# Spectral components stored from GpSimd's queue and read back behind their own store, and one block of matmuls moved ahead of the transposes

## Chip, cores and metric

One Trainium2 chip, one core. The time is that of the device in microseconds, from an execution's start to its end; the span in a profile leaves out some 2 us of that. Each kernel has several executions, and one of them is profiled. In the trace of the kernel before, TensorE does the matmuls (5826) and leaves their sums in the buffer PSUM; VectorE (679 instructions), ScalarE (487) and GpSimd (114) work on tiles; SyncE only issues transfers (the 14 stores of 512 KB among them), and ScalarE (4 stores of 256 KB) and GpSimd (8 stores of the filter) issue some too.

## The reference

```python
x = A_x                                             # 2048 x 1024, bf16
x = x + irfft2(rfft2(layernorm(x)) * (w_r + 1j*w_i))  # spectral layer
x = x + mish(layernorm(x) @ w1 + b1) @ w2             # dense layer, 1024 -> 3584 -> 1024
x = x + irfft2(rfft2(layernorm(x)) * (w_r + 1j*w_i))
x = x + mish(layernorm(x) @ w1 + b1) @ w2
```

## The kernel before

The transforms are matmuls with tables. A spectral layer works in 8 groups of frequencies. Stage s2 and s3 go forward, then comes the filter, then i1 and i2 go back. Each group leaves 128 x 16 x 128 components (512 KB) in a buffer U. The last transform, i4, needs them with all groups side by side in the partitions, so each group's U is stored to memory and read back in another order, in 256-byte pieces (2048 packets a group in the trace). A transfer is issued by an engine's queue. SyncE's works in its program's order: in experiment 5 it stood for 5 us until a store had landed, with the next store behind it.

```python
def u_turn(g, half):                      # after i2 of (group, half)
    u = U[g % 3]
    if g == 7:                            # last group, in two halves, ScalarE's queue
        h = slice(8 * half, 8 * half + 8)
        if half == 0:
            u_back(6)
        self.dma(act, self.u_d[g][:, h, :], u.ap[:, h, :], ...)
        if half:
            u_last()                      # read-backs of group 7 in six pieces, SyncE and ScalarE
    elif half:
        self.dma(sp, self.u_d[g], u.ap, ...)      # store, SyncE's queue
        if g:
            u_back(g - 1)                         # read-back of the group before, SyncE's queue
...
def layer_B(...):
    for u in range(4):
        self.i4(0, 4, 32 * u, 32, 2 * u)  # last transform, four quarters of 32 matmuls
        ...                               # ScalarE moves the sums from PSUM, VectorE takes statistics
    rest(0)                               # postponed block of 15 matmuls, PSUM banks 0 to 2
    for j in range(2):
        xn[j] = self.apply(j)             # VectorE normalises two tiles
    for j in range(2):
        transposed(0, j, xn[j])           # TensorE transposes, VectorE copies
    self.warm(ACT.Mish)                   # ScalarE loads a table (1.28 us)
    rest(3)                               # second block of 15, banks 3 to 5
    ...
        mm1(0, fg, 0, ...)                # dense matmuls
```

Of the kernel before, what the change touches and what calls it, by code (L numbers as in the profile page):

```python
# [179 lines left out]
class KB:  # L180
# [508 lines left out]
    def layer_A(self, li):  # L689
# [7 lines left out]
        dve, act, sp, pool = self.dve, self.act, self.sp, self.pool  # L697
# [166 lines left out]
        def u_turn(g, half):  # L864

            u = U[g % 3]
            if g == 7:
                h = slice(8 * half, 8 * half + 8)
                if half == 0:
                    u_back(6)  # L870
                self.dma(act, self.u_d[g][:, h, :], u.ap[:, h, :], f"uwh{half}", reads=[u.res], writes=[self.r_ud7[half]])
                if half:
                    u_last()
            elif half:
                self.dma(sp, self.u_d[g], u.ap, f"uw{g % 3}", reads=[u.res], writes=[self.r_ud[g]])
                if g:
                    u_back(g - 1)

        def open_ut():
            self.UT = self.alloc("UT", o["UT"], [P, P])  # L880

            self.r_ut = self.sub_res(self.UT, "ut", 4, o["UT"], P * P * 2)
            for r in self.r_ut:
                r.begin()

        def u_back(g):
            if self.UT is None:
                open_ut()
            self.dma(sp, self.UT.ap[g:P:8, :, :], self.u_d[g].rearrange("l r n -> r l n"), f"usp{g % 3}",
                     reads=[self.r_ud[g]], parts=self.r_ut)  # L890

        def u_last():

            def back(prog, half, q, n):
                l = slice(32 * q, 32 * q + 32 * n)
                self.dma(prog, self.UT.ap[7 + 64 * half:P if half else 64:8, l, :], self.u_d[7][l, 8 * half:8 * half + 8, :].rearrange("l r n -> r l n"),
                         f"ul{half}{q}", reads=[self.r_ud7[half]], parts=self.r_ut[q:q + n])
            back(sp, 0, 0, 2)
            back(sp, 0, 2, 2)
            for q in range(4):  # L900
                back((act, sp)[q % 2], 1, q, 1)
# [13 lines left out]
        for stage, g, h in self.order_A():  # L915
            if stage == 2:
                s2(g, h)
                if li == 0 and h == 0:
                    filter_bins(g)
                    if g in (0, 1):  # L920
                        load_w(g + 4)
                    elif g in (4, 5):
                        load_w(g + 2)
            elif stage == 3:
                s3(g, h)
                if h:
                    if g < 6:
                        load_tabs(g + 2)
                    if li == 0:
                        self.keep_filter(g)  # L930
                    elif g < 4:
                        load_w(g + 4)
            elif stage == 4:
                i1(g, h)
                if h and g < 6:
                    load_btabs(g + 2)
            else:
                i2(g, h)
                u_turn(g, h)
# [109 lines left out]
    def layer_B(self, li, last):  # L1049
        pe, dve, act, sp, pool = self.pe, self.dve, self.act, self.sp, self.pool  # L1050
# [109 lines left out]
        def at_tiles(c):  # L1160
            off = self.ob[f"AT{c}"]
            AT[c] = self.alloc(f"AT{c}", off, [NF, 512])
            r_at[c] = [Res(f"AT{c}_{ft}") for ft in range(NF)]
            for ft, r in enumerate(r_at[c]):
                r.inherit(AT[c].res)
                self.live.append((off + ft * 1024, off + ft * 1024 + 1024, r))

        def rest(bank, n=15, prog=act):

            u0 = self.u0  # L1170
            self.u0 += n
            self.i4(4, 12, u0, n, bank)
            self.i4_out(4, 12, u0, n, bank, staged=YS, prog=prog)
# [17 lines left out]
            self.out_first(u, 2, (act, act, act, dve)[u])  # L1191
        self.root(0, 2)
        rest(0)
        for j in range(2):
            xn[j] = self.apply(j)
        for j in range(2):
            transposed(0, j, xn[j])
        self.warm(ACT.Mish)
        rest(3)
        at_tiles(0)  # L1200
        for j in (2, 3):
            self.stats_dve(j)
# [118 lines left out]
```

## Time and profile before

| | before |
|---|---|
| time, first three runs | 1014.44, 1014.7, 1017.05 us |
| TensorE busy, share of the span | 95% |
| GpSimd busy | 8% |
| granted TensorE clock, mean | 0.992 |
| stores of 512 KB (SyncE's queue), to landing | 3.8 us |

The times of equal runs differ by 2.6 us. TensorE ran two stretches of together 17 us at half clock in this trace (granted clock 0.50 from 116.64 to 123.47 and from 604.75 to 614.99 us). The page's list of DMA issues has, for each kind of transfer, queue, count, size and median time from issue to landing:

```profile
u_scratch<-ARENA SPq DMA_DIRECT2D x14, 512.0 KB, 3.8
ARENA<-u_scratch SPq DMA_DIRECT2D x14, 512.0 KB, 6.1
```

TensorE's timeline at the first layer's turn (start, duration, line, shape, count; in brackets the idle time before and what ended it):

```profile
113.56 0.95 PE L1014 MATMUL PS<-MT,ARENA 128*128 128x32 bf16 x32 [1.62 <-DMA ARENA<-u_scratch]
115.35 2.88 PE L1014 MATMUL PS<-MT,ARENA 128*128 128x32 bf16 x96 [0.83 <-DMA ARENA<-u_scratch]
119.89 1.38 PE L1014 MATMUL PS<-MT,ARENA 128*128 128x96 bf16 x15 [1.67 <-ACT XS L568]
```

TensorE waits 1.67 us for ScalarE, and runs the first postponed block.

### The profile page before, as it was taken

To read this page: it belongs to the slowest core of one execution; us is meant where nothing else is said; L and a number is where in the kernel's file an instruction comes from. 1 tells how busy PE (TensorE), PEld (TensorE's weight loads), DVE (VectorE), ACT (ScalarE), POOL (GpSimd) and SP (SyncE) were. 2 spreads that over 40 slices of the span, in tenths; PEclk is the share of its full clock that TensorE was granted. 3 is DMA by queue.
4 is the path that set the end of the run, shared out by engine and by line. 5 is a ranking of instruction groups with operands and counts; after the bars stand their busy time and mean duration, and the time that the engine had idled before them with its cause. 6 is when DMAs were issued, how large, how long until landed. Compare 5 with 4: busy or idle time off the path is not lost.

```text
span 1013.4 us, 13752 instructions
## 1 busy us (share of the span) xinstructions
PE 958.2 (95%) x5826; PEld 506.4 (50%) x5826; DVE 326.5 (32%) x679; ACT 347.7 (34%) x487; POOL 81.5 (8%) x114
## 2 busy tenths in 40 slices
PE   0799799999999999999999979999999999999998
PEld 0667575444444444444456748644444444444443
DVE  6797568002444000033347736830011100000111
ACT  7798474440000443300029837534100023430000
POOL 3831000000000000002421100000000000000000
PEclk9999899999999999999999998999999999999999
DMA  9969823652111220002922875246411212100000
GB/s 281 281 191 321 213 60 115 198 196 65 48 46 32 74 82 21 1 21 85 199 60 84 232 187 154 77 161 203 129 25 45 73 52 83 43 1 11 21 27 26
DMA packets 154205, 107.00 MB, mean 106 GB/s; under 512 B 74448, under 2 KB 133664, under 8 KB 154144
## 3 DMA queue, kind: packets, MB, share of 16 engines
q1 hardware_dynamic: 143056, 78.61, 27.5%
q0 software_dynamic: 8912, 25.84, 8.7%
q10 hardware_dynamic: 2176, 1.66, 0.5%
q8 instruction: 47, 0.77, 0.3%
q14 instruction: 14, 0.11, 0.0%
HBM read 80.85 MB, written 20.71 MB: 100 GB/s over the span
## 4 chain that ended last, share of the span: by engine, by line
PE 87%; DVE 5%; DMA 4%; ACT 2%; POOL 1%; issue 0%; SPq 0%; ACTq 0%; POOLq 0%; DVEq 0%
PE PS L1121 38%; PE PS L1103 38%; PE PS L793 2%; PE PS L719 2%; PE PS L1014 2%; PE PS L818 2%; DMA XS<-in_A_x_dram 1%; DMA ARENA<-c_bt 1%; POOL ARENA L249 1%; PE PS L1069 1%; DMA ARENA<-u_scratch 1%; DVE ARENA L637 1%; DMA u_scratch<-ARENA 1%; DVE ARENA L775 1%; DVE ARENA L610 1%; ACT ARENA L635 1%
## 5 line engine op out<-in xcount | busy, mean ns | idle before, releaser
L1103 PE MATMUL PS<-ARENA 128*128 128x512 bf16 (+1 forms) x1984 | 390.9, 358 | 0.2
L1121 PE MATMUL PS<-ARENA 128*128 128x512 bf16 x1792 | 387.4, 379 | 0.0
L1107 ACT ACTIVATE ARENA<-PS,B 128x512 bf16<-128x512 f32 (+1 forms) x248 | 159.4, 645 | 411.6 <-PE PS L1103 411.0
L1103 PEld LDWEIGHTS PS<-ARENA 128*128 128x128 bf16 x1984 | 193.0, 98 | 192.7 <-DVE ARENA L1074 0.9
L1121 PEld LDWEIGHTS PS<-ARENA 128*128 128x128 bf16 x1792 | 175.4, 98 | 211.4
L1132 DVE TENSOR_TENSOR XS<-PS,XS 128x512 bf16<-128x512 f32 x63 | 43.6, 692 | 582.3 <-PE PS L1121 582.3
L460 DVE BATCH_NORM_STATS2 BN<-XS 128x6 f32<-128x512 bf16 x99 | 63.8, 673 | 6.1 <-DMA XS<-in_A_x_dram 5.1
L249 POOL DMA_DIRECT2D xn_scratch<-ARENA x12 | 6.5, 541 | 373.4 <-DVE ARENA L512 373.4
L793 PE MATMUL PS<-ARENA 128*128 128x256 bf16 x256 | 32.4, 273 | 3.9 <-DVE ARENA L782 3.2
L771 ACT ACTIVATE ARENA<-PS 128x1024 bf16<-128x1024 f32 x32 | 33.3, 1071 | 4.5 <-PE PS L767 4.5
L432 ACT ACTIVATE RS<-MV,EPS 128x2 f32<-128x2 f32 (+2 forms) x5 | 1.5, 297 | 96.6 <-DVE MV L463 84.4
L719 PE MATMUL PS<-FD,ARENA 128*128 128x256 bf16 (+1 forms) x256 | 31.8, 271 | 2.4 <-ACT ARENA L635 1.2
L1014 PE MATMUL PS<-MT,ARENA 128*128 128x32 bf16 (+1 forms) x512 | 22.3, 201 | 9.7 <-DMA ARENA<-u_scratch 6.3
L804 ACT ACTIVATE ARENA<-PS 128x1024 bf16<-128x1024 f32 x28 | 29.8, 1087 | 3.9 <-PE PS L793 3.9
L793 PEld LDWEIGHTS PS<-ARENA 128*128 128x128 bf16 x256 | 24.0, 98 | 12.0 <-DVE ARENA L782 5.7
L568 ACT ACTIVATE ARENA<-PS 128x1440 bf16<-128x1440 f32 (+1 forms) x22 | 25.5, 1160 | 10.8 <-PE PS L793 3.9
L775 DVE TENSOR_TENSOR ARENA<-ARENA 128x1024 bf16<-128x1024 bf16 x32 | 22.0, 688 | 19.8 <-ACT ARENA L771 19.8
L719 PEld LDWEIGHTS PS<-FD,ARENA 128*128 128x128 bf16 x256 | 24.4, 98 | 6.5 <-DVE ARENA L637 1.4
L1014 PEld LDWEIGHTS PS<-MT,ARENA 128*128 128x128 bf16 x512 | 20.6, 104 | 12.7 <-issue 7.2
L818 PE MATMUL PS<-ARENA,BD 128*128 128x256 bf16 x192 | 24.9, 273 | 1.6 <-DVE ARENA L572 1.6
L862 ACT ACTIVATE ARENA<-PS 128x1024 bf16<-128x1024 f32 x24 | 25.3, 1090 | 0.0
L512 DVE TENSOR_SCALAR ARENA<-XS,MV,RS 128x1024 bf16<-128x1024 bf16 x47 | 24.3, 543 | 0.9
(85 smaller groups left out, 530.6 us busy)
## 6 DMA issues: line engine op xcount, KB each, us to landing
ARENA<-in_B_w_dram SPq DMA_DIRECT2D x56, 512.0 KB, 3.9
ARENA<-in_B_w_dram SPq DMA_DIRECT2D x56, 256.0 KB, 4.3
u_scratch<-ARENA SPq DMA_DIRECT2D x14, 512.0 KB, 3.8
ARENA<-u_scratch SPq DMA_DIRECT2D x14, 512.0 KB, 6.1
w_scratch<-ARENA POOLq DMA_DIRECT2D x8, 512.0 KB, 6.9
ARENA<-w_scratch POOLq DMA_DIRECT2D x8, 512.0 KB, 5.3
out_dram<-XS SPq DMA_DIRECT2D x16, 256.0 KB, 2.1
ARENA<-xn_scratch POOLq DMA_DIRECT2D x15, 256.0 KB, 9.1
```

The source lines that it names most:

```text
L460: self.op(self.dve, lambda e: e.bn_stats(self.BN[:, j, 6 * h:6 * h + 6], self.XS[:, j, 512 * h:512 * h + 512]), reads=[self.r_xs[j]], part ...
L719: fns.append(lambda e: e.matmul(dst, at(r), FD[:, t:t + n], start=start, stop=stop))
L771: self.op(act, lambda e: e.activation(x.ap.rearrange("p a b -> p (a b)"), ps, ACT.Copy, scale=SIG), reads=banks, writes=[x.res])
L775: self.op(dve, lambda e: e.tensor_tensor(ta.ap, x.ap, wt.ap[:, 0:1, :].to_broadcast([P, 2, 512]), ALU.mult), reads=[x.res, wt.res], writes ...
L793: fns.append(lambda e, c=c, part=part: e.matmul(ps[:, c * 256:(c + 1) * 256], yk.ap[:, part, c * P:(c + 1) * P], t[:, (128, 0)[part]:(384, ...
L804: self.op(act, lambda e: e.activation(v.ap[:, :, i, :], src, ACT.Copy), reads=banks, parts=[v.res])
L818: fns.append(lambda e, dst=dst, part=part, c=c: e.matmul(dst, BD[:, c:c + P], mov(kd, part), start=(part == 0), stop=(part == 1)))
L1014: fns.append(lambda e, l=l: e.matmul(self.PS[:, bank + l // k, l % k * w:(l % k + 1) * w], self.UT.ap[:, u0 + l, :], self.MT[:, 8 * lo:8 * ...
L1103: fns.append(lambda e, db=db, bank=bank, fl=fl: e.matmul(PS[:, bank, 0:w], wb.ap[:, db, fl * P:(fl + 1) * P], x.ap[:, db, tok], start=(db ...
L1107: self.op(act, lambda e, bank=bank, ft=ft: e.activation(at.ap[:, ft, tok], PS[:, bank, 0:w], ACT.Mish, bias=self.B1[:, ft:ft + 1]), reads= ...
L1121: fns.append(lambda e, i=i, ft=ft: e.matmul(PS[:, bank, :], at.ap[:, ft, t * P:(t + 1) * P], W2[ft].ap[:, h * 512:(h + 1) * 512], start=(i ...
L1132: self.op(dve, lambda e: e.tensor_tensor(xs, PS[:, bank, :], xs, ALU.add), reads=[self.r_bank[bank]], writes=[self.r_xs[j]])
```

## The change

Its intent: take the stores off SyncE's queue, so that a read-back can wait for its own store there without holding the next store, and have read-backs done a group earlier. And fill TensorE's wait for the normalised tile with the second postponed block.

```diff
             if g == 7:
                 h = slice(8 * half, 8 * half + 8)
-                if half == 0:
-                    u_back(6)
                 self.dma(act, ...)
             elif half:
-                self.dma(sp, self.u_d[g], u.ap, f"uw{g % 3}", reads=[u.res], writes=[self.r_ud[g]])
-                if g:
-                    u_back(g - 1)
+                self.dma(pool, self.u_d[g], u.ap, f"uw{g % 3}", reads=[u.res], writes=[self.r_ud[g]])
+                u_back(g)
@@ layer_B
         rest(0)
+        rest(3)
         for j in range(2):
             xn[j] = self.apply(j)
         for j in range(2):
             transposed(0, j, xn[j])
         self.warm(ACT.Mish)
-        rest(3)
```

## The prediction

> **What bounds the kernel now.** I read the page first. TensorE is busy 95% of the span, and the chain that ended last runs on it for 87%, mostly in the two dense layers (L1103, L1121). The change touches only the two spectral layers, about 37 to 124 us and 522 to 615 us of the span. So the question is which waits of TensorE stand there.
>
> ```profile
> span 1013.4 us, 13752 instructions
> PE 958.2 (95%) x5826; PEld 506.4 (50%) x5826; DVE 326.5 (32%) x679; ACT 347.7 (34%) x487; POOL 81.5 (8%) x114
> PE 87%; DVE 5%; DMA 4%; ACT 2%; POOL 1%; issue 0%; SPq 0%; ACTq 0%; POOLq 0%; DVEq 0%
> ```
>
> DMA is 4% of the chain, some 40 us, of which the first load of the input is 11.6 us. Next, the TensorE timeline of the first spectral layer between 60 and 100 us. Only two of its waits are for a transfer, both loads on GpSimd's queue:
>
> ```profile
> 76.04 0.62 PE L975 MATMUL PS<-ARENA 128*128 128x256 bf16 x4 [0.36 <-DMA ARENA<-in_A_w_i_dram]
> ...
> 79.34 1.03 PE L793 MATMUL PS<-ARENA 128*128 128x256 bf16 x8 [0.71 <-DMA ARENA<-c_bt]
> ```
>
> The chain prints 9.41 us for that table load, but TensorE idled only 0.71 us; the rest of the load lay beside matmuls. In the second spectral layer the same timeline has no wait for a transfer between 537 us and the turn. Then the chain in order of time, at that layer's turn, the passage into the dense layer:
>
> ```profile
> 597.09 4.01 DMA u_scratch<-ARENA
> 601.10 0.02 issue
> 601.12 4.37 DMA ARENA<-u_scratch
> 605.49 0.14 issue
> 605.62 3.59 PE PS L1014 x128
> ...
> 611.82 0.56 DVE ARENA L512
> 612.38 0.05 issue
> 612.42 1.89 PE PS L1069 x16
> 614.31 1.01 PE PS L1014 x15
> 615.33 1.75 PE PS L1103 x16
> ```
>
> Here transfers set the end: the last group's store (4.01 us), its read-back (4.37 us), then the last transform (L1014), the normalisation, transposes (L1069), one postponed block of 15 matmuls (L1014) and the first dense matmuls (L1103). From there TensorE works without a transfer wait to the end of the dense layer, so a microsecond gained or lost at L1103 stays.
>
> Why 4 us for a store of 256 KB? The DMA view of a narrow window, 596.9 to 598.0 us, shows it. The store was issued on ScalarE's queue (q10) at 596.03 for its first half and 597.09 for its second:
>
> ```profile
> q1 hardware_dynamic: 893, 0.23, 130.9%
> q10 hardware_dynamic: 1, 0.00, 0.8%
> ```
>
> Queue 1 is SyncE's, and its packets are the 256-byte pieces of the read-backs of groups 5 and 6. One ScalarE packet passed. Only from 598 on does q10 move (145 packets in the next microsecond). The store of group 7 stands behind SyncE's backlog for a good microsecond.
>
> [...] GpSimd's queue does alternate with SyncE's between 71 and 78 us. [...] 512 KB on an otherwise quiet engine took 2.6 us from SyncE (issued at 61.75 us) and 3.5 us from GpSimd (59.12 us, with a 192 KB load just ahead). [...] granted clock 0.50 from 116.64 to 123.47 us and from 604.75 to 614.99 us[...]. Both half-clock stretches cover the transposes.
>
> **Part A: the store moves to GpSimd, the read-back follows its own store.** Nothing is removed and no size changes. In each layer 7 stores of 512 KB change queue, and 7 read-backs of 512 KB move: each was issued behind the next group's store, and is now issued when its own has landed. A store costs GpSimd 0.54 us of issue (all its plain issues take 0.53 to 0.57), 7 x 0.54 = 3.8 us per layer on an engine that is 8% busy.
>
> Middle of the first layer: store 0 is ready at 61.75 us and its read-back is issued only at 68.38, behind store 1, in front of the filter and table loads that TensorE later waits for. The windows view has DMA at 4 GB/s from 64 to 68 us: idle. After the change the store lands near 65 and the read-back runs in that hole (until about 70). Ahead of the critical table load GpSimd's queue then has 512 KB of filter and the 512 KB of store 1: with its own 192 KB, 1.2 MB at about 300 GB/s (the 306 GB/s of 60 to 64 us) is 4 us after 69.8, so it lands about 75.5 instead of 79.2. Both waits go: 0.36 + 0.71 = **-1.1 us**. In the second layer this gains nothing.
>
> Turn, in each layer: store 6 on SyncE took 3.1 us (591.03 to 594.14), sharing its queue with read-back 5. From GpSimd, from its quiet 256 KB store of 2.4 us plus 0.64 us for 256 KB more (64 packets of 4 KB at 159 ns over 16 engines), about 3.0 us. Read-back 6 can't start sooner than that, so it is issued at the same time as now, within 0.1 us. What it saves is standing behind read-back 5: 1.3 us to its first packet, then 2048 packets at 18 ns over 16 engines, 2.3 us, so its last packet goes at 594.0 + 3.6 = 597.6 rather than 598.3. Store 7 gets in up to 0.6 us sooner; some of that goes where read-back 5, now issued near 589, still overlaps store 6. I take **-0.4 us per layer, -0.8 us**.
>
> **Part B: the postponed block goes ahead of the transposes.** Same instructions, new order. Now TensorE does block 1 (610.87 to 612.05, 15 x 80 ns at half clock), idles a little, transposes from 612.42 when the normalised tile comes, then block 2 while VectorE copies the transposed tile (0.69 us), and the first dense matmul at 615.16. After it, block 2 is between: 612.05 + 1.2 = 613.25; 16 transposes x 107 ns at half clock end at 614.96; 0.3 us latency and VectorE's second copy of 0.69 us end at 615.9; dense matmul 615.95, +0.8 us. In the first layer: transposes from 122.27, the clock rises at 123.47, last one at about 123.7, copy done at 124.6, dense matmul 124.68 against 124.12, +0.55 us. The block filled TensorE's time while VectorE copied; moved, it fills a gap of only 0.4 us before the transposes and leaves the copy uncovered. At full clock it would cost about nothing, as 2 x 0.64 us fit before the tile is ready. ScalarE's copies of both blocks now come before its table load instead of around it, with the same end for the first dense activation. Sum **+1.35 us**.
>
> **Sum.** -1.1 - 0.8 + 1.35 = -0.55 us, from a median of 1014.7: about 1014.2 us.
>
> **Rivals.** First, GpSimd's queue is in order, so a store that waits for its data holds the loads behind it: the table load after store 2, issued at 73.72 now, would be issued at about 78.9 and land at about 82.2, against a need at about 85.5; in the second layer it lands near 574 against 576.9. For it: before, the same loads took 5.6 to 9.4 us in busy stretches, which would eat these 3 us. Against: the read-backs no longer fall there. It would make 1 to 3 us more: 1015 to 1017. Second, store 7 is held not by the packets left but by SyncE's last issues as such; then a drained backlog frees it wholly, both turns gain up to 2 us (598.1 less the 596.9 at which it could have started, and faster landing), and the time is 1011 to 1012. Against: read-back 6 still waits for store 6, which comes no sooner. [...] Fourth, all of A is hidden and only B shows: 1016.
>
> **Range and chances.** The rivals reach from 1011 to 1017, the least likely at the ends; the three runs of before spread from 1014.44 to 1017.05. Range 1012.0 to 1016.4. Two per cent is 20 us, most of the transfer time on the chain after the input's load; nothing here comes near it, so 0.99 for within 2%, and the rest split.
>
> **What would show it.** Right: no wait on a transfer in front of L975 and L793 near 76 to 80 us; table load landing by 76; read-backs issued 3 to 4 us after their own stores; q10's packets starting about 0.5 us sooner after their issue; in the turn, L1014 x30 unbroken, then L1069, then a gap of about 0.9 us before L1103. Wrong: a wait of L793 on the table load of group 5 (86 us or 576 us), a store of group 6 slower than 3.5 us, or no gap before L1103.

## The result

The four runs took 1014.32, 1017.02, 1017.1 and 1017.27 us, median 1017.06; the kernel before beside them 1014.44, 1014.7, 1014.86 and 1017.05. The ratio is 1.0011, with an interval from 0.9989 to 1.0034: the same. The forecast of no change within 2% held. The median of these four, though, lies above the 1016.4 that I gave as the upper end; in the next timing of the same kernel it was 1015.83.

The page after, DMA issues:

```profile
u_scratch<-ARENA POOLq DMA_DIRECT2D x14, 512.0 KB, 4.3
ARENA<-u_scratch SPq DMA_DIRECT2D x14, 512.0 KB, 5.9
```

A store lands half a microsecond later in the median. (Three code lines went away, so L1014 is now L1011, L1069 is L1066, L1103 is L1100.) TensorE's timeline, in the middle of the first layer and at its turn:

```profile
85.15 1.91 PE L793 MATMUL PS<-ARENA 128*128 128x256 bf16 x16 [0.44 <-DMA ARENA<-c_bt]
...
114.27 3.72 PE L1011 MATMUL PS<-MT,ARENA 128*128 128x32 bf16 x128 [3.69 <-DMA ARENA<-u_scratch]
119.66 1.45 PE L1011 MATMUL PS<-MT,ARENA 128*128 128x96 bf16 x30 [1.67 <-ACT XS L568]
121.22 1.08 PE L1066 MATMUL PS<-IDENT,ARENA 128*128 128x128 bf16 x16
```

The two waits at 76 and 79 us are gone. A new one of 0.44 us, for the table of group 5, has come; the next trace of the same kernel (e1_again) doesn't have it. At the turn i4 no longer starts in two pieces: all 128 matmuls wait, 3.69 us. The block of 15 is one of 30, and the transposes follow without a gap. The chain in order of time at the second turn:

```profile
596.17 3.65 DMA u_scratch<-ARENA
599.82 0.02 issue
599.84 4.19 DMA ARENA<-u_scratch
604.03 0.14 issue
604.16 0.97 PE PS L1011 x32
605.13 0.03 issue
605.16 2.67 PE PS L1011 x96
607.83 0.02 issue
607.86 1.58 ACT XS L568 x3
609.44 0.05 issue
609.49 2.58 PE PS L1011 x30
612.07 0.87 PE PS L1066 x8
612.93 0.02 issue
612.96 1.30 DVE ARENA L1071 x2
614.26 0.05 issue
```

Store and read-back are 0.36 and 0.18 us shorter than before. But VectorE's copy of the transposed tiles (L1071, 1.30 us) now stands in the chain, where the second block had covered it.

### Reading a change that is smaller than the noise

Whole times differ by up to 6.3 us between runs of one kernel (1013.05 to 1019.31 in experiment 4), so I cut each trace at marks and compare the parts. The marks are starts of instructions in the timeline: the layer's first s2 matmul (L719); ScalarE's issue of the first half of store 7; the first matmul of the postponed block. The "middle" is from the first to the second mark, the "turn" from the second to the third. Outside these and the stretch after the block, parts repeat closely: from the first layer's second dense product to the second layer's first s2 matmul it is 306.80 to 306.87 us in all traces.

| trace | stores | block | middle 1 | turn 1 | sum 1 | middle 2 | turn 2 |
|---|---|---|---|---|---|---|---|
| before | old | old | 66.12 | 13.71 | 79.83 | 60.30 | 14.84 |
| e7_before_again | old | old | 66.08 | 13.70 | 79.78 | 60.30 | 14.80 |
| e3_only_block | old | moved | 66.01 | 13.59 | 79.60 | 60.29 | 14.93 |
| e11_block_again | old | moved | 66.01 | 13.93 | 79.94 | 60.30 | 15.17 |
| changed | new | moved | 65.32 | 14.85 | 80.17 | 60.30 | 14.37 |
| e1_again | new | moved | 64.72 | 14.79 | 79.51 | 60.29 | 15.07 |
| e2_only_stores | new | old | 64.72 | 14.42 | 79.14 | 60.29 | 14.44 |
| e6_hybrid | hybrid | old | 65.28 | 13.46 | 78.74 | 60.30 | 14.77 |
| e12_hybrid_again | hybrid | old | 64.72 | 15.00 | 79.72 | 60.30 | 15.05 |
| e9_hybrid_block | hybrid | moved | 65.33 | 13.95 | 79.28 | 60.30 | 14.72 |

(Experiment 4, with its filler matmuls, is left out of both tables: middle 65.25 us, turns 15.04 and 13.92, and 111.86 and 404.20 us in the stretch of the second table.)

The store change takes 1.1 us out of the middle of the first layer (mean 66.06 to 64.92), and the turn behind it gives 1.0 back (13.73 to 14.69). The sum goes from 79.79 to 79.61. The second layer's turn gains 0.3 (14.94 to 14.63). The middle with moved stores has two values: near 65.3 us where L793 waits 0.41 to 0.45 us for the table of group 5, and 64.72 where it doesn't. The changed kernel and the hybrid (experiment 6) each have both among their traces.

The stretch from the postponed block on, in the traces of the kernels above and of the experiments e5, e8 and e10 (block where it was): in the first layer to the first matmul of the second dense product, in the second layer to the end of the span.

| block | traces | first layer, mean (range) | second layer, mean (range) |
|---|---|---|---|
| where it was | 8 | 109.35 (108.99 to 110.14) | 402.76 (402.46 to 402.96) |
| moved | 5 | 109.77 (108.33 to 111.90) | 402.82 (401.79 to 403.25) |

### The profile page after: what moved, and what is told of

Its sections match the earlier page's. It is cut to its first block, busy times and chain, and to the rows that moved or that the text cites. A ratio compares the mean times of both kernels' runs of the same rounds, so it can differ in the third digit from the quotient of the medians.

```text
span 1012.5 us, 13667 instructions
## 1 busy us (share of the span) xinstructions
PE 951.8 (94%) x5742; PEld 505.4 (50%) x5826; DVE 326.2 (32%) x679; ACT 347.5 (34%) x487; POOL 89.5 (9%) x128
## 3 DMA queue, kind: packets, MB, share of 16 engines
q0 software_dynamic: 10928, 33.18, 10.5%
## 4 chain that ended last, share of the span: by engine, by line
PE 86%; DVE 5%; ACT 4%; DMA 3%; issue 1%; SPq 0%; ACTq 0%; POOL 0%; DVEq 0%
PE PS L1118 38%; PE PS L1100 38%; PE PS L719 2%; PE PS L1011 2%; PE PS L793 2%; PE PS L818 1%; ACT ARENA L441 1%; DMA ARENA<-u_scratch 1%; DVE ARENA L637 1%; DMA XS<-in_A_x_dram 1%; DMA u_scratch<-ARENA 1%; DVE ARENA L610 1%; PE PS L1066 1%; ACT ARENA L754 1%; DVE ARENA L775 1%
## 5 line engine op out<-in xcount | busy, mean ns | idle before, releaser
L1100 PE MATMUL PS<-ARENA 128*128 128x512 bf16 (+1 forms) x1950 | 389.1, 358 | 3.7 <-DVE ARENA L1071 1.8
L1100 PEld LDWEIGHTS PS<-ARENA 128*128 128x128 bf16 x1984 | 193.0, 98 | 194.6 <-DVE ARENA L1071 2.8
L793 PE MATMUL PS<-ARENA 128*128 128x256 bf16 x256 | 32.3, 273 | 3.6 <-DVE ARENA L782 3.2
L719 PE MATMUL PS<-FD,ARENA 128*128 128x256 bf16 (+1 forms) x256 | 31.8, 271 | 2.4 <-ACT ARENA L635 1.2
L1011 PE MATMUL PS<-MT,ARENA 128*128 128x32 bf16 (+1 forms) x512 | 21.3, 199 | 10.4 <-DMA ARENA<-u_scratch 7.0
L793 PEld LDWEIGHTS PS<-ARENA 128*128 128x128 bf16 x256 | 24.0, 98 | 11.8 <-DVE ARENA L782 4.7
L719 PEld LDWEIGHTS PS<-FD,ARENA 128*128 128x128 bf16 x256 | 24.4, 98 | 6.5 <-DVE ARENA L637 1.4
L1011 PEld LDWEIGHTS PS<-MT,ARENA 128*128 128x128 bf16 x512 | 19.9, 102 | 13.3 <-issue 8.8
```

Of the source, the lines that this page charges most:

```text
L719: fns.append(lambda e: e.matmul(dst, at(r), FD[:, t:t + n], start=start, stop=stop))
L793: fns.append(lambda e, c=c, part=part: e.matmul(ps[:, c * 256:(c + 1) * 256], yk.ap[:, part, c * P:(c + 1) * P], t[:, (128, 0)[part]:(384, ...
L1011: fns.append(lambda e, l=l: e.matmul(self.PS[:, bank + l // k, l % k * w:(l % k + 1) * w], self.UT.ap[:, u0 + l, :], self.MT[:, 8 * lo:8 * ...
L1100: fns.append(lambda e, db=db, bank=bank, fl=fl: e.matmul(PS[:, bank, 0:w], wb.ap[:, db, fl * P:(fl + 1) * P], x.ap[:, db, tok], start=(db ...
```

## The experiments

### 1. The same kernel again

No edit.

> The changed kernel itself, again. The first timing had one run at 1014.3 us (granted clock 0.995) and three near 1017.1 us (0.990 to 0.992). Theory 1 (half-clock windows at the two turns[...]): again two clusters some 2.7 us apart, the lower clock always in the longer runs, and both kernels show both clusters. Theory 2 (the change itself is 2 us slower and the first run was a lucky one): nearly all runs near 1017, the kernel before near 1014.7.

Measured: six runs from 1013.08 to 1017.61 us, median 1015.83; the kernel before, 11 runs, 1013.62 to 1017.4, median 1015.12. Ratio 1.0000 (0.9986 to 1.0015). The six runs in order of time, with their granted clock: 1013.08 (0.995), 1014.34 (0.993), 1015.46 (0.992), 1016.2 (0.992), 1016.24 (0.990), 1017.61 (0.988).

What follows: theory 2 falls, and so do the two clusters of theory 1, as the times fill the whole stretch. The longer runs have the lower clock, and from 0.995 to 0.988 there are 14 us more at half clock (an estimate: 0.007 x 1014 x 2, at a granted clock of 0.50), where 4.5 us are lost. That lower clock and longer time go together is shown here; in the kernel before they go together less closely (0.992 came with 1014.33 and with 1017.4).

The traces show one regularity. In each of the 14, all half-clock stretches start on one grid of 3.413 us through the whole span: in the kernel before the second starts 143.00 steps after the first (116.64 and 604.75 us), in the changed kernel 144.00 (114.68 and 606.20 us). The stretches there are 6.83 and 10.24, and 3.41 and 6.83 us long, which is one to three steps. Where that grid lies against the span differs from trace to trace.

### 2 and 3. Each part alone

Part A alone (e2): the block put back.

```diff
         rest(0)
-        rest(3)
         ...
         self.warm(ACT.Mish)
+        rest(3)
```

> Part A alone: stores on GpSimd's queue and read-backs behind their own stores, the postponed block where it was. My prediction has A at -1.9 us (mid layer -1.1, turns -0.4 each), so about 1012.8 and 1.3 us faster than the changed kernel in the same clock state. From the changed trace I now expect less: mid layer -1.07 + 0.44 (the new wait on the table load of group 5) = -0.6, second turn -0.5, first turn 0, so about 1013.6. Rival: the gain of A is eaten by the slower store of group 6 (5.1 us in the first layer), then 1014.7 or more.

Measured: 1015.52 us median, ratio 1.0003 (0.9990 to 1.0017). Middle 64.72 us, turns 14.42 and 14.44. The gain in the middle is there (1.4 us in this trace), the loss at the first turn too (0.7), so the rival came true in part. The whole is the same as before.

Part B alone (e3): the kernel before with the block moved.

```diff
         rest(0)
+        rest(3)
         ...
         self.warm(ACT.Mish)
-        rest(3)
```

> Part B alone: the block of 15 moved ahead of the transposes, stores and read-backs as before. My prediction: +0.55 us in the first turn and +0.8 in the second, 1.35 us slower than before, about 1016.0, and a gap of about 0.9 us of TensorE in front of the first dense matmul where there was none. Rival (clock): [...] the cost is 0 or 2 to 3 us from run to run. Rival (B is free): 1014.7, with the block inside the wait for the normalised tile.

Measured: 1015.35 us median, from 1013.47 to 1019.3, ratio 1.0001 (0.9984 to 1.0019). The profiled run was the quickest, with the clock at half only from 114.00 to 117.41 and from 605.52 to 608.93 us. TensorE's timeline at its first turn:

```profile
119.47 1.45 PE L1014 MATMUL PS<-MT,ARENA 128*128 128x96 bf16 x30 [1.67 <-ACT XS L568]
121.02 1.08 PE L1069 MATMUL PS<-IDENT,ARENA 128*128 128x128 bf16 x16
123.03 1.16 PE L1103 MATMUL PS<-ARENA 128*128 128x256 bf16 x9 [0.93 <-DVE ARENA L1074]
```

At full clock both blocks fit in front of the normalised tile, and from block to first dense matmul it takes 3.56 us. The gap of 0.93 us is where I expected it. Nothing was lost there in this run, and the expectation of 1016.0 missed; that the cost depends on the clock (the first rival) fits.

### 4. TensorE kept busy in front of the read-backs

```diff
-        self.spin(4, 0)
+        self.spin(18, 0)          # filler matmuls, results unused
         self.residual_first()
```

> The changed kernel with 18 instead of 4 filler matmuls (results unused, 0.216 us each at full clock) ahead of the residual matmuls at each turn, so that TensorE works until just before the last read-back lands: 3.0 us of work into a gap of 3.7 (first turn) and 3.3 us (second). If the half-clock windows come from that gap, the clock stays at or near 1.0 there, the longer cluster vanishes and the time is about 1013 in all runs; the granted clock of the runs is above 0.995. If they come from the later gap (1.7 us, waiting for ScalarE) or the thin block of 32-column matmuls, nothing changes. If the filler delays the residual past the landing, up to +0.5 us per turn.

Measured: 1013.05 to 1019.31 us, median 1015.38, ratio 1.0005 (0.9986 to 1.0024). The idle time in front of i4 went from 3.7 to 0.31 us in the first layer. Four runs had a clock of 0.995 to 0.998 and took 1013.05 to 1015.77 us; two had 0.991 and took 1017.97 and 1019.31. In the profiled one, a long run, the clock fell at 118.07 us, after the thin i4 matmuls, and stayed at half for 10.24 us, into the dense matmuls.

What follows: the filled gap is not all that decides. In this run the half-clock stretch moved later, and from the postponed block on the first layer took 111.86 us (109.77 in the mean of the moved block); the expectation of 1013 in all runs failed. The grid of experiment 1 says more. Over the 14 traces, from some 27 us of the span on, 42 of its steps stand just before a fall to half clock, and TensorE was busy for 0 to 0.66 of them; 39 stand just before a rise, and it was busy for 0.79 to 1.00 of those (in the kernel before 0.66 and 0.13 ahead of the falls at 116.64 and 604.75 us, 0.95 ahead of both rises). Here the step before the fall, 114.66 to 118.07 us, holds most of the thin matmuls and the start of the wait for ScalarE, and TensorE is busy for 1.94 us of it (0.57). But full-clock steps in which it was busy for only 0.42 were also followed by full clock, so the busy share alone doesn't settle it.

### 5. The order without the queue

Against the changed kernel:

```diff
-                self.dma(pool, self.u_d[g], u.ap, ...)
+                self.dma(sp, self.u_d[g], u.ap, ...)
                 u_back(g)
```
(and the block where it was)

> Order alone: each read-back directly behind its own store, but the stores on SyncE's queue as before, the postponed block where it was. SyncE then waits 2.6 to 3.2 us at each read-back before it can go on. Theory (order does the work, good and bad): first spectral layer from its first s2 matmul to the issue of the last group's store 65.0 us (before 66.1, 66.0), store 6 lands 5 us after its issue because read-back 5 is in front of it, and the turn from that issue to the postponed block takes 14.5 to 15 us in the first layer (before 13.7, 13.6). Rival (queue does it): store 6 at 3.1 us and the first turn at 13.6, and the waits of 0.36 and 0.71 us in the middle may stay.

Measured: 1022.81 us median against 1015.7, ratio 1.0062 (1.0046 to 1.0078), 7 us longer in the medians. SyncE's queue, timeline at the first turn:

```profile
101.60 1.38 SPq L249 DMA_DIRECT2D u_scratch<-ARENA  x1
106.61 0.54 SPq L249 DMA_DIRECT2D ARENA<-u_scratch  x1
107.19 1.22 SPq L249 DMA_DIRECT2D u_scratch<-ARENA  x1
112.26 4.52 SPq L249 DMA_DIRECT2D ARENA<-u_scratch  x5
```

Store 6 is issued at 107.19 us, after ScalarE has issued the first half of store 7 (104.60 us), because SyncE stood 5 us waiting for store 5 to land. The turns take 19.4 and 19.1 us. The middle of the first layer is 64.72 us, as short as with the whole change.

What follows: the gain in the middle comes from the order alone. But with the stores on SyncE's queue it costs 7 us more than it brings; on GpSimd's (part A alone) it does not. My theory, that order does all, was wrong on that.

### 6. The change without its harm

```diff
-                self.dma(pool, self.u_d[g], u.ap, f"uw{g % 3}", ...)
-                u_back(g)
+                self.dma(sp if g == 6 else pool, self.u_d[g], u.ap, "uws6" if g == 6 else f"uw{g % 3}", ...)
+                if g != 5:
+                    for b in ((5, 6) if g == 6 else (g,)):
+                        u_back(b)
```
(and the block where it was)

> The store change without its harm: groups 0 to 5 store on GpSimd's queue, read-backs 0 to 4 behind their own stores, but store 6 on SyncE's queue and read-back 5 behind it, as before; the block where it was. Theory: middle of the first layer 65.0 us as with the change, store 6 back to 3.1 us, first turn back to 13.65 us, second turn 14.9 us, so 1.0 us better than before in the sum of parts and about 1014.0 in the mean of runs, which the clock's noise of 1.5 us a run can hide. Rival (store 6 was slow because the GpSimd path is slow when SyncE's queue is full, and read-back 4 is enough for that): store 6 above 4 us again, first turn above 14.3.

Measured: 1014.82 us median against 1015.7, ratio 0.9991 (0.9977 to 1.0005). Middle 65.28 us, turns 13.46 and 14.77. Store 6, from the DMA views of narrow windows, in the changed kernel and here:

```profile
u_scratch<-ARENA POOLq DMA_DIRECT2D x1, 512.0 KB, 5.1
```
```profile
u_scratch<-ARENA SPq DMA_DIRECT2D x1, 512.0 KB, 3.2
```

And the start of i4 in two pieces is back:

```profile
112.76 0.95 PE L1013 MATMUL PS<-MT,ARENA 128*128 128x32 bf16 x32 [1.64 <-DMA ARENA<-u_scratch]
114.55 2.59 PE L1013 MATMUL PS<-MT,ARENA 128*128 128x32 bf16 x96 [0.84 <-DMA ARENA<-u_scratch]
```

What follows: putting store 6 in front of read-back 5 again takes away the harm of the first turn in this trace. It also takes store 6 off GpSimd's queue, so by itself it doesn't refute the rival (GpSimd's path). Experiment 5 speaks against it: there store 6, on SyncE's own queue behind read-back 5, took 5.05 us.

### 7. The kernel before, one more trace

No edit.

> The kernel before, for another trace. The parts that depend on no clock repeat: 66.1 us in the middle of the first layer, turn 13.7 us in the first layer and 14.9 in the second; only the start (input load, up to 1 us) and the stretch from the postponed block to the first dense matmul move: 4.2 to 4.5 us at half clock, as in the first trace, or near 3.6 us if the clock is full there. 3.6 at full clock would say that moving the block gains nothing even then, as the moved one also took 3.56 us.

Measured: 1015.41 us. Middle 66.08, turns 13.70 and 14.80, as expected. From block to dense matmul 4.45 and 4.44 us, with the transposes at half clock again. No trace with the block where it was had full clock all through this stretch, so what the old order takes at full clock is left open; the nearest is the second layer of experiment 12, at full clock for the first 2.2 us, with 3.94 us.

### 8. Read-back 6 behind all others

```diff
                 self.dma(pool, self.u_d[g], u.ap, ...)
-                u_back(g)
+                if g < 6:
+                    u_back(g)
@@ u_last
             for q in range(4):
                 back((act, sp)[q % 2], 1, q, 1)
+            u_back(6)
```
(and the block where it was)

> Stores on GpSimd's queue, read-backs 0 to 5 behind their own stores, read-back 6 put behind all read-backs of group 7; the block where it was. If the store of group 7's second half is held by the packets of read-back 6 (3.1 to 3.6 us in the changed traces, 2.1 for the first half when nothing is in front), it now lands about 2.2 us after its issue in both layers. The data to move is the same, so the last landing should hardly move: first turn 14.0 to 14.7 us, second 14.0 to 14.5. Rival (the turn's length is latency in a chain, not packets in front): the last landing comes 1 us or more sooner, turns of 13.5.

Measured: 1022.46 us median, ratio 1.0065 (1.0049 to 1.0081). The first half of store 7, first layer:

```profile
u_scratch<-ARENA ACTq DMA_DIRECT2D x1, 256.0 KB, 2.0
```

It is 2.0 us for both halves in the first layer, and 2.06 and 1.97 in the second, against 3.64 and 3.1, 4.44 and 4.0 before. So the stores of group 7 do stand behind the packets of read-back 6, by up to 2.4 us. The rest of the expectation failed: the last landing came much later, turns of 18.2 and 18.5 us. Between 113 and 116 us the read-backs together moved 119 GB/s, less than the 128 GB/s of group 7's alone in the kernel before (111 to 115 us). With 512 KB more to bring at that rate the turn grows by some 4 us (an estimate from these rates). Packets of 256 bytes don't set that rate by themselves: from 99 to 100 us of the changed kernel, read-back 5 alone moved 286 GB/s. Why the rate is lower here, I have not settled.

### 9. The hybrid with the moved block

Experiment 6, with the block moved as in experiment 3.

> The hybrid (middle of the layer as changed, stores 6 and read-backs 5 and 6 as before) together with the moved block: candidate for the best. From the parts: middle of the first layer 65.0 to 65.3 us, turns 13.5 and 14.8 us. From the block to the first dense matmul: so far 4.2 to 4.5 us in all unmoved cases; moved 3.56 us where the clock was full (3 of 8) and 4.2 to 5.1 where it was half. Theory (the moved block costs 0.3 to 0.7 us at half clock but lets the clock stay full more often, so it is worth nothing on the mean): time within 0.5 us of the hybrid alone, some 0.7 us under the kernel before. Rival (prediction: B costs about 0.65 us a turn): 1.3 us slower than the hybrid.

Measured: 1016.11 us median, 1013.2 to 1017.27, ratio 0.9993 (0.9978 to 1.0008). By ratio it is within 0.2 us of the hybrid, as the theory has it; by median it is 1.3 us slower, as the rival has it. With intervals of 1.5 us to each side the times don't decide. Its trace has half-clock stretches of 13.65 and 10.24 us, in sum as long as the longest of the others (experiments 5 and 10), against the second half of the theory: in this trace the moved block does not keep the clock up. Moved, the stretch after the block has been the shortest (108.33) and the longest (111.90).

### 10. A filter's store out of the way

```diff
-                        self.keep_filter(g)
+                        if g < 7:
+                            self.keep_filter(g)
...
+        if li == 0:
+            self.keep_filter(7, self.r_ut)    # issued when all read-backs have landed
         self.spin(4, 0)
```
(part A alone otherwise)

> Part A alone, with the last 512 KB store of the filter of the first layer (issued on GpSimd's queue just after store 5) held back until all read-backs have landed. Theory (store 6 lands late in the first layer because the data engines are behind: the filter's store and read-backs 4 and 5 are in front of it): store 6 in 4.0 us or less instead of 5.2, first turn from the last group's store to the postponed block 13.9 us or less instead of 14.4 to 14.9; the second layer, which has no such store, stays at 14.4 to 15.1. Rival (store 6 waits only for the packets of read-back 5, which is issued when store 5 lands, whatever else moves): store 6 at 5.0 us or more and the first turn unchanged.

Measured: 1016.14 us median, ratio 0.9999 (0.9980 to 1.0019). Store 6 in 3.7 us instead of 5.3, as expected; the first turn 14.40 us, as long as in e2. So the backlog in front of store 6 is cleared, and yet the turn isn't shorter. Read-back 6 now is issued 1.1 us ahead of store 7, whose first half takes 3.99 us again, and the last landing comes 10.3 us after that store's issue (10.0 before). The clock was at half from 116.39 us on (116.64 in the kernel before), and also from 37.88 to 44.71 us, which makes its middle (66.48 us) of no use. Inconclusive on the turn.

### 11. Part B alone, one more trace

> Part B alone, for another trace of the stretch from the postponed block to the first dense matmul. In its first trace both turns ran at full clock and took 3.56 us. At half clock I expect 4.5 to 5.1 us; at full clock 3.56 again. The middle of the first layer 66.1 us and the turns 13.6 and 14.9 us, as in the kernel before.

Measured: 1017.65 us. Middle as in the kernel before, turns 0.2 and 0.3 us longer (13.93 and 15.17). From block to dense matmul 4.23 us in the first layer, with the block at full clock and the transposes at half, and 4.73 us in the second at half clock. In the first layer the half clock then lasted to 127.92 us, and the whole stretch took 110.96 us, 2.6 us more than in e3. Same program, same place: the clock makes 2.6 us of difference.

### 12. The hybrid again

No edit against experiment 6.

> The hybrid without the moved block, again, because its first timing (0.9991, interval 0.9977 to 1.0005) left open whether it beats the kernel before. From the parts: middle of the first layer 65.0 to 65.3 us against 66.0 to 66.1, both turns as before (13.5 to 13.7 and 14.8 to 14.9 us), so 0.9 us less, a ratio of 0.9991. Rival (its gain is noise): the middle of the first layer at 66 us, or a ratio of 1.000. With a spread of 1.5 us a run, the ratio alone may again not tell.

Measured: 1015.4 us median against 1015.76, ratio 0.9990 (0.9976 to 1.0003). Middle 64.72 us, but the first turn 15.00, with store 6 in 3.4 and read-back 5 in 6.5 us. So the hybrid too can give the gain of the middle back at the turn; its sum in three traces is 78.74, 79.28 and 79.72 us, against 79.60 to 79.94 with the old stores. Two timings agree on 0.1% less, and neither is clear of nothing. It is the best candidate, and not proven.

## Why the prediction was right, and where not

- **No change within 2%**: right, for the reason given: nothing that the change touches holds more than a few microseconds.
- **Part A, middle of the first layer, -1.1 us**: right in cause, and in size (66.06 to 64.92) partly by luck: it was 1.3 us in the two traces without the new wait and 0.7 in the one with it. Read-back 0 went into the hole (issued 64.44, landed 71.59 us), the table load landed at 75.62, both waits went. (The estimate was 75.5, but 4 us after 69.8 is 73.8; the prediction doesn't say where the rest comes from.) The first rival came true in part: GpSimd's queue issued store 2 at 78.38 us, after a wait of 5.16, and the load behind it only at 79.44 (73.72 before); it landed at 85.01, not 82.2, and cost the 0.44 us. Experiment 5 shows that it is the order that gains.
- **Part A, second turn, -0.4 us**: right, -0.3 in the means, with store 6 at 3.1 to 3.3 us (about 3.0 predicted), though e1's own 15.07 shows a spread as large.
- **Part A, first turn, -0.4 us**: wrong, it was +1.0. The step that failed is "From GpSimd ... about 3.0 us" for store 6, and with it that read-back 6 "is issued at the same time as now, within 0.1 us". Store 6 took 5.1 us, and read-back 6 was issued 5.16 us after it instead of 3.16. I had priced a quiet engine, and had taken the turn's other numbers from the second layer and carried them to the first. In the second layer of the changed kernel, read-back 5 is issued 2.9 us ahead of store 6, and its packets go on for about 1 us beside it; in the first it is 2.0 us ahead, and they go on for about 3. In the changed kernel, read-back 5 is ahead of store 6 and not behind it. DMA view of the changed kernel, 100.6 to 102.7 us, GpSimd's store having been issued at 100.00:

```profile
q1 hardware_dynamic: 1709, 0.44, 131.2%
q0 software_dynamic: 1, 0.00, 0.9%
```

  SyncE's 256-byte packets go, and of the store one packet. (Part of that is the store's own start: GpSimd's store at 61.44 us, with nothing in front, had its first packet after 1.1 us; this one after 2.6.) VectorE doesn't explain it: in experiment 10 it ran the same instructions beside store 6, which took 3.7 us. I had seen the same between SyncE's and ScalarE's queues, and had then trusted that GpSimd's "does alternate" (266 packets of its queue and 2031 of SyncE's from 71 to 78 us of the kernel before).

  Two things follow at the turn: the second half of store 7 stands behind read-back 6 (3.5 us; its first half, now in front of it, took 2.2), and the piece that i4's first quarter needs lands about 9 us after store 7's issue instead of 7.1 (but 8.3 in experiment 11, with the old stores), so that i4 starts whole and late. The last landing hardly moves (10.2 to 10.5 us after store 7's issue instead of 9.8 to 10.1).

  Experiment 6 undid the order for groups 5 and 6 alone, and all of this with it in its trace; with the same order i4 again started whole in experiments 9 and 12. Experiments 10 and 12 show that this isn't the whole: store 6 in 3.7 and 3.4 us still had turns of 14.4 and 15.0. It fits that the transfers, not TensorE, set the end of the first layer, and that a TensorE which comes sooner waits longer. The traces support this: from the layer's first s2 matmul, the last read-back lands after 75.8 to 76.2 us with the old stores and 75.1 to 75.8 with new and hybrid ones, and among these it is the same whether the middle took 64.72 us (mean 75.4) or 65.3 (75.4). So of the 1.1 us gained in the middle about 0.7 reach the last landing. No experiment changed the transfers' own rate, so the cause of the loss stays argued in part.
- **The signs**: of the three that were to show the prediction wrong, two came, L793's wait for the table of group 5 and a store of group 6 slower than 3.5 us, both in the first layer. Of those for right, read-backs followed their stores by 3.0 to 5.6 us there, not 3 to 4.
- **The clock**: the grid step before the first fall of the kernel before, 113.23 to 116.64 us, wasn't idle: TensorE was busy for 2.24 us of it. What makes the clock fall isn't shown here.
- **Part B, +0.55 and +0.8 us**: right in mechanism (gap of 0.93 and 0.83 us behind the transposes, the block no longer covering VectorE's copy) and too large in size. Where the clock was at half for all or most of it, from block to dense matmul it was 4.2 to 5.1 us moved (mean 4.75) against 4.2 to 4.5 (mean 4.39); but where the clock was full it took 3.56. In the means over the whole stretch B is +0.4 and +0.1 us, with a spread of 3.6 us. The term mis-sized is "16 transposes x 107 ns at half clock", taken as certain from the one trace that I had.
- **The sum, -0.55 us**: from the parts it is about -1.1 + 1.0 - 0.3 + 0.5 = 0.1 us. The ratios, 1.0011 and 1.0000, agree and can't tell more.
- **The range**: too narrow for a median of four runs. The spread of a single run is over 4 us, and I had taken the 2.6 us of three.

## What to carry to other kernels

A transfer moved earlier can come to stand ahead of one that others wait for (here read-back 5 ahead of store 6, which took 5.1 us instead of 3.1): list what is in front of each transfer on the path, before and after. A read-back that waited directly behind its store held the later stores of the same queue (7 us of the kernel's time in experiment 5). And where the clock moves single runs by more than the change is worth (2.6 us in experiment 11), cut the traces at marks and compare the parts, in several traces of each kernel.
